# Attention and two MLPs on one core: first loads cut by columns, key parts written straight into the stacked operand, other half copied

## Chip, cores, metric

The kernel runs on one core of one Trainium2 chip. The metric is the device time of one execution in microseconds (us). The four compute engines have queues of their own that run in order: TensorE (PE), VectorE (DVE), ScalarE (ACT) and GpSimd (POOL); SyncE (SP) and ACT issue the DMAs.

## What is computed

The reference, cut to what matters (two batches, eight heads, 576 positions, head size 64):

```python
q_rot, k_rot = rotate(q), rotate(k)            # rotary position encoding, half = 32
scores = scale * q_rot @ k_rot.T               # scale = 1/8
attn = softmax(scores)                          # max subtracted first
x = (attn @ v) as [1152 tokens, 512]
h = x @ w_in;  x = (h * sigmoid(h)) @ w_out     # 2048 wide
for e in range(4):                              # 1024 wide each
    out += p[:, e] * (relu(x @ w1[e]) @ w2[e])
```

## The kernel before

All of the output has to be close to float32. A product is therefore made from two parts of each factor: a high part (the value rounded to the matmul's input type, `F32R`) and a low part (the value less its high part).

**Pairs and units.** Attention is worked in eight pairs of heads. A pair's rotated keys and queries lie as `xk` and `xq` with head 0 on partitions 0 to 63 (`TOP`) and head 1 on 64 to 127 (`LOW`). A pair has nine units (four blocks of 128 queries for each head, and one block for the rest of both). A unit is: `scores` into a PSUM tile `s` of which there are two; `rowmax` on DVE; `expo` on ACT; four to six transposes on PE (`transp`), copied out of PSUM by ACT, or by DVE for the units named in `EVD`; then `av` in two halves of a pair, and `norm`.

**The stacked operand.** `scores` uses `KK` and `QQ`, two of each, for pairs in turn. `QQ` holds a head's query high part on partitions 0 to 63 and its low part on 64 to 127; `KK[:, 0]` holds the key's high part on both halves of the partitions and `KK[:, 1]` its low part. So two accumulating matmuls over 128 partitions give all products of parts. The parts were first made in tiles of their own (`k2` by `key_high` on ACT and `key_low` on DVE, `q2` by `query_high` and `query_low` on POOL), and DMAs then spread them: four of 288 KB a pair into `KK` (`key_spread`, L275) and four of 144 KB into `QQ` (`query_spread`, L291), all from SP.

**The first units.** Before the first pair's stacked operand is there, its first `NUN` = 5 units use `first_scores` (L349): two plain float32 matmuls on the 64 partitions of one head, straight from `xq` and `xk`.

**Order.** It is written out by hand: `START` lists the steps ahead of the loop, `LATE` those put at a half step of it, and the loop has one step for each of the 72 units, in which `ORDER0` (first pair), `ORDER` and `ORDER2` (last two pairs) give the order of atoms: S scores and M rowmax of the unit two ahead, E exponential of the next, T and H transposes, L the DVE copy, B the `av` and `norm` work named in `PLAN`, W and w pieces of a weight conversion (`WIDE`). `OFF`, `OFF1` (pair 1) and `OFF2` (pair 2) give the half step at which each pair's preparation is put: `lk`, `lq`, `lv` loads; `k1` to `k3` and `q1` to `q3` the rotary; `k4`, `k5`, `q4`, `q5` the parts. `DV0` and `DV1` say which of these run on DVE and not on POOL in the first two pairs.

Ahead of everything PE runs 13 matmuls on a zero tile (L956). The MLPs follow the attention; the change leaves their code as it is.

Of the kernel before, what the change touches and what calls it, by code (L numbers as in the profile page):

```python
# [11 lines left out]
ALU = mybir.AluOpType  # L12
AX = mybir.AxisListType

PLAN = [['L0'], ['L1'], ['Ln'], [], ['P0'], [], [], ['P1', 'Pn'], []]
PLAN0 = [[], [], [], [], [], ['P0'], ['P1'], ['Pn'], []]
PLAN2 = [['L0'], [], ['L1', 'Ln'], [], ['P0'], [], [], [], ['P1', 'Pn']]
ORDER = ['vSEVTwMHXWBL', 'SBTHEwvVXWML', 'SMvXVEwTHWBL', 'vBSWTVEMHXLw', 'STVHMEwBvXWL', 'SVvEwXMWTBHL', 'ETSVwvMHXWLB', 'VTSMvWHEXLBw', 'SWTEHXvMLwBV']
ORDER0 = ['XETSHvWVMBLw', 'SVETXwMvBWHL', 'TwSvHWEXBVLM', 'SvXMWVTBHLEw', 'TVvHBXWSMwEL', 'vVEXBwSTHLWM', 'EvTHLSWwBVMX', 'VTSEvHMBLWwX', 'WwXSTBHMELvV']
ORDER2 = ['SvEMXTBHLWVw', 'vWSTMBHLEwXV', 'TvXESwWVMHLB', 'BEvSTVXMHWwL', 'TWVwSMHLEBvX', 'VELXwSBvWTMH', 'TEwBSHXvVMLW', 'TSHLEVMwWvXB', 'vBESMVWTHXwL']  # L20
WIDE = [[6, 10, 12, 14, 16, 17, 19], [18, 22, 24, 26, 28, 29, 32], [32, 35, 37, 39, 42, 44, 46], [42, 46, 48, 50, 51, 52, 55]]
# [4 lines left out]
OFF = {'k1': -28, 'k2': -27, 'k3': -25, 'k4': -19, 'k5': -16, 'q1': -20, 'q2': -26, 'q3': -19, 'q4': -18, 'q5': -14, 'lk': -42, 'lq': -35, 'lv': -5}  # L26
OFF1 = {'k1': 4, 'k2': 4, 'k3': 6, 'k4': 6, 'k5': 6, 'q1': 0, 'q2': 4, 'q3': 5, 'q4': 6, 'q5': 7, 'lv': 10}
OFF2 = {'k1': 8, 'k2': 6, 'k3': 14, 'k4': 17, 'k5': 18, 'q1': 9, 'q2': 15, 'q3': 15, 'q4': 19, 'q5': 23, 'lk': 2, 'lq': 5, 'lv': 31}
DV1 = ['k1', 'k2', 'q1', 'q2', 'q3']
DVR = []  # L30
EVD = [1, 3, 8, 4]
FIRST = [0, 2, 1, 3, 4, 5, 6, 7, 8]
NUN = 5
START = ['ka', 'kb', 'qa', 's0', 'h', 's1', 'c1', 'c2', 'm0', 'l', 'qb', 'c3', 'ch', 'x0', 's2', 'm1', 'cl']
LATE = {'d': 0, 'e': 0, 'gh': 1, 'gl': 1, 'k0': 0, 'k1': 0, 'q0': 2, 'q1': 2}
DV0 = ['c1', 'c2', 'd', 'e']
# [10 lines left out]
def fused_kernel(ctx, tc, q, k, v, w_in, w_out, dprobs, w1, w2, cst, out):  # L47
# [198 lines left out]
    def rotary(P, nm, g, rows=ALL, cols=FULL):  # L246
        x = getattr(P, "x" + nm)[rows, :, cols]

        def times(z, tab):
            if P.n == 0 and nm == "k":  # L250
# [17 lines left out]
    def key_low(P, rows=ALL, cols=FULL):  # L268
        nc.vector.scalar_tensor_tensor(P.k2[rows, 1, cols], P.xk[rows, 0, cols], 0.125 if P.n else 1.0,
                                       f32(P.k2)[rows, 0, cols], ALU.mult, ALU.subtract)  # L270

    def key_spread(P, heads=(0, 1)):
        for h in heads:
            for a in range(2):
                nc.sync.dma_start(f32(KK[P.i][64 * a:64 * a + 64, :, 576 * h:576 * h + 576]),  # L275
                                  f32(P.k2[64 * h:64 * h + 64, :, :]))
            made.add((P, "k", h))
# [9 lines left out]

    def query_spread(P, heads=(0, 1), cols=FULL):
        for h in heads:
            for z in range(2):  # L290
                nc.sync.dma_start(f32(QQ[P.i][64 * z:64 * z + 64, 640 * h + cols.start:640 * h + cols.stop]),  # L291
                                  f32(P.q2[64 * h:64 * h + 64, z, cols]))
            made.add((P, "q", h))
# [14 lines left out]
    def scores(P, un):  # L308
        hf, r, h = un
        if P.n == 0 and P.units.index(un) < NUN:  # L310
            return first_scores(P, un)
        for x in ("k", "q"):
            for h_ in (0, 1) if h == 2 else (h,):
                assert (P, x, h_) in made
# [22 lines left out]
    def first_scores(P, un, nbs=(0, 1)):  # L337
# [586 lines left out]
    def attention():  # L924
# [6 lines left out]
        QA, QB, QC, QD = slice(0, 128), slice(128, 256), slice(256, 576), slice(0, 256)  # L931
        P0.xk = yp.tile([128, 2, 576], F32, name="xk")
        P0.xq = yp.tile([128, 2, 576], F32, name="xq")
        parts(P0, "k")
        parts(P0, "q")

        def load0(e, dst, src, rows, cols=FULL):
            e.dma_start(dst[rows, :, cols], src[0, 0, rows, :, cols])

        def table0(rows, cols=FULL):  # L940
            nc.scalar.dma_start(TAB[rows, :, cols], TABS[rows, :, cols])
# [37 lines left out]
        def eng(name):  # L979
# [4 lines left out]
            "ka": all_of(rotary(P0, "k", V, TOP, CA)), "kb": all_of(rotary(P0, "k", V, TOP, CB)),  # L984
            "qa": all_of(rotary(P0, "q", V, TOP, QA)),
            "h": lambda: key_high(P0, TOP), "l": lambda: key_low(P0, TOP),
            "c1": lambda: rotary(P0, "k", eng("c1"), LOW)[0](), "c2": lambda: rotary(P0, "k", eng("c2"), LOW)[1](),
            "c3": lambda: rotary(P0, "k", eng("c3"), LOW)[2](),
            "ch": lambda: key_high(P0, LOW), "cl": lambda: key_low(P0, LOW),
            "qb": all_of(rotary(P0, "q", eng("qb"), TOP, QB)),  # L990
            "d": all_of(rotary(P0, "q", eng("d"), LOW, QD)),
            "e": all_of(rotary(P0, "q", eng("e"), ALL, QC)),
            "gh": lambda: query_high(P0, g), "gl": lambda: query_low(P0, eng("gl")),
            "k0": lambda: key_spread(P0, (0,)), "k1": lambda: key_spread(P0, (1,)),
            "q0": lambda: query_spread(P0, (0,)), "q1": lambda: query_spread(P0, (1,)),
# [8 lines left out]
        def prepare(Z):  # L1004
# [8 lines left out]
            its["k4"] = lambda: (parts(Z, "k"), key_high(Z))  # L1013
            its["k5"] = lambda: (key_low(Z), key_spread(Z))
            its["q4"] = lambda: (parts(Z, "q"), query_high(Z, g))
            its["q5"] = lambda: (query_low(Z, nc.vector if "q5" in dve else g), query_spread(Z))
            its["lv"] = lambda: load_v(Z)
            at = {1: OFF1, 2: {a: n - 36 for a, n in OFF2.items()}}.get(Z.n, OFF)
            for a in ("lk", "lq", "lv", "k1", "k2", "k3", "k4", "k5", "q1", "q2", "q3", "q4", "q5"):
# [10 lines left out]
        need = ["lk<k1", "lk<k2", "k1<k3", "k2<k3", "k3<k4", "k4<k5", "lq<q1", "lq<q2", "q1<q3", "q2<q3", "q3<q4", "q4<q5"]  # L1030
        for Z in range(1, NPAIR):
# [3 lines left out]
            for a, b in (("k5", "k4"), ("q5", "q4")):  # L1035
                assert order.get((Z - 1, a), -1) <= order[Z, b]
# [3 lines left out]
            if Z > 1:  # L1040
                for a in ("k5", "q5"):
                    assert order[Z, a] > 18 * Z - 24
# [202 lines left out]
```

## Time and profile before

| | |
|---|---|
| three runs | 755.44 us median, 754.74 to 756.63 |
| profiled execution | 755.87 us, of which the span of the trace is 754.1 us |
| PE busy | 740.4 us, 98% of the span |
| DVE, ACT, POOL busy | 472.5, 302.5, 263.4 us |
| granted TensorE clock, mean | 0.981 of 2.4 GHz |
| attention | from 0 to about 160 us |

The page lists busy time of each engine, its share in 40 equal slices of the span, the granted clock of PE in the same slices, the chain of work that ended last, and groups of instructions by source line. Line numbers are those of the kernel before. Of an engine that is busy 98% of the time, the places to read are the slices where it isn't, and those in which its clock was lower. Durations below are of one profiled execution.

### The profile page before, as it was taken

The page shows a single profiled execution, that of the slowest core. Times are in us where ns is not written, and L with a number is a line of the kernel's source. Part 1 is how long each engine was busy: PE and PEld are TensorE (multiplying, and loading weights), DVE is VectorE, ACT ScalarE, POOL GpSimd, SP SyncE. Part 2 cuts the span into 40 slices and gives each one's busy share as a digit, 9 for nine tenths or more (in the row PEclk, how much of TensorE's full clock was granted, in tenths as well). Part 3 has the DMA queues.
Part 4 walks back from the last instruction along what each step waited for, and adds up shares of the span by engine and source line. Part 5 has one row for each costly group of instructions (what it writes and reads, how often), then busy time and mean ns, then how long its engine had stood idle before and what let it go on. Part 6 is the DMA issues. An engine that isn't in the chain of part 4 may idle for free.

```text
span 754.1 us, 11327 instructions
## 1 busy us (share of the span) xinstructions
PE 740.4 (98%) x4398; PEld 667.3 (88%) x4398; DVE 472.5 (63%) x878; ACT 302.5 (40%) x679; POOL 263.4 (35%) x256
## 2 busy tenths in 40 slices
PE   6999999999999999999999999999999999999998
PEld 5667777779999999999998998989989899898996
DVE  6557878667999897984574544545445454464542
ACT  2457777664425335243242331413314133242330
POOL 2748878411003103026312614226152261522600
PEclk7789999999999999999999999999999999999999
DMA  8877686611233131330110300203012030110002
GB/s 224 215 207 195 180 244 173 165 60 31 83 112 112 57 111 57 107 118 1 56 56 1 98 16 23 91 1 108 4 34 79 1 110 3 45 68 0 2 29 99
DMA packets 26759, 63.65 MB, mean 84 GB/s; under 512 B 3536, under 2 KB 4048, under 8 KB 26704
## 3 DMA queue, kind: packets, MB, share of 16 engines
q1 hardware_dynamic: 25008, 61.91, 27.2%
q10 hardware_dynamic: 1696, 1.00, 0.7%
q8 instruction: 35, 0.57, 0.3%
q14 instruction: 20, 0.16, 0.1%
HBM read 46.39 MB, written 2.36 MB: 65 GB/s over the span
## 4 chain that ended last, share of the span: by engine, by line
PE 91%; DMA 3%; DVE 2%; POOL 2%; issue 1%; ACT 0%; POOLq 0%; DVEq 0%
PE m L766 9%; PE m L765 9%; PE m L767 9%; PE m L694 7%; PE m L693 7%; PE m L692 7%; PE m L576 5%; PE m L577 4%; PE m L578 4%; PE m L601 4%; PE m L600 4%; PE m L599 4%; PE b L440 4%; PE s L323 4%; PE b L296 4%; PE m L649 1%
## 5 line engine op out<-in xcount | busy, mean ns | idle before, releaser
L771 DVE SCALAR_TENSOR_TENSOR acc<-m,dp,acc 128x512 f32<-128x512 f32 (+1 forms) x64 | 47.5, 742 | 108.1 <-PE m L767 108.1
L766 PE MATMUL m<-wl,gh 128*128 128x512 f32 (+1 forms) x292 | 113.1, 387 | 0.0
L765 PE MATMUL m<-wh,gh 128*128 128x512 f32 (+1 forms) x292 | 113.0, 387 | 0.0
L767 PE MATMUL m<-wh,gl 128*128 128x512 f32 (+1 forms) x292 | 112.7, 386 | 0.0
L713 DVE SCALAR_TENSOR_TENSOR gl<-g,gh 128x288 fp32r<-128x288 f32 x84 | 50.7, 603 | 45.0 <-ACT gh L712 43.2
L675 POOL TENSOR_TENSOR wl<-raw,wh 128x512 fp32r<-128x512 f32 x21 | 27.2, 1298 | 141.9 <-ACT wh L672 141.9
L588 POOL TENSOR_TENSOR gl<-g,gh 128x384 fp32r<-128x384 f32 x24 | 26.8, 1120 | 142.7 <-ACT gh L587 142.6
L356 DVE TENSOR_REDUCE nm<-s 128x1 f32<-128x576 f32 x72 | 54.0, 750 | 32.8 <-PE s L323 20.9
L694 PE MATMUL m<-xh,wl 128*128 128x288 f32 x224 | 66.1, 295 | 0.0
L693 PE MATMUL m<-xl,wh 128*128 128x288 f32 x224 | 66.0, 294 | 0.0
L692 PE MATMUL m<-xh,wh 128*128 128x288 f32 x224 | 65.9, 294 | 0.0
L767 PEld LDWEIGHTS m<-wh,gl 128*128 128x128 f32 x292 | 54.8, 188 | 11.3
L366 ACT ACTIVATE p<-s,nm 128x576 f32<-128x576 f32 x72 | 53.7, 746 | 27.2 <-DVE nm L356 26.3
L765 PEld LDWEIGHTS m<-wh,gh 128*128 128x128 f32 x292 | 54.8, 188 | 10.6
L599 PE MATMUL m<-gh,wh 128*128 128x384 f32 x192 | 64.1, 334 | 0.0
L600 PE MATMUL m<-gh,wl 128*128 128x384 f32 x192 | 64.1, 334 | 0.0
L601 PE MATMUL m<-gl,wh 128*128 128x384 f32 x192 | 64.1, 334 | 0.0
L766 PEld LDWEIGHTS m<-wl,gh 128*128 128x128 f32 x292 | 54.8, 188 | 10.3
L675 POOL TENSOR_TENSOR wl<-cvt,wh 128x512 fp32r<-128x512 f32 x28 | 36.2, 1294 | 69.7 <-ACT wh L672 69.7
L672 ACT CAST wh<-cvt 128x512 fp32r<-128x512 f32 x28 | 17.4, 621 | 89.4 <-DVE cvt L671 89.4
L323 PE MATMUL s<-kk,qq 128*128 128x288 f32 x236 | 48.5, 329 | 3.5 <-DMA qq<-q 3.3
L693 PE MATMUL m<-tf,wh 128*128 128x288 f32 x168 | 49.6, 295 | 0.0
(142 smaller groups left out, 1883.1 us busy)
## 6 DMA issues: line engine op xcount, KB each, us to landing
raw<-in_moe_w_dram SPq DMA_DIRECT2D x16, 1024.0 KB, 5.1
kk<-k SPq DMA_DIRECT2D x32, 288.0 KB, 4.7
raw<-in_moe_w_out_dram SPq DMA_DIRECT2D x8, 1024.0 KB, 4.9
raw<-in_moe_w_in_dram SPq DMA_DIRECT2D x6, 1024.0 KB, 5.2
qq<-q SPq DMA_DIRECT2D x32, 144.0 KB, 4.5
xk<-in_k_dram SPq DMA_DIRECT2D x7, 576.0 KB, 5.4
xq<-in_q_dram SPq DMA_DIRECT2D x7, 576.0 KB, 6.7
xv<-in_v_dram SPq DMA_DIRECT2D x8, 320.0 KB, 5.3
```

Source lines behind the costliest of these rows:

```text
L323: nc.tensor.matmul(s[:, nb, 0:288], lq, kk[:, a, c:c + 288], start=(a == 0), stop=(a == 1))
L356: nc.vector.tensor_reduce(P.nm[:, c:c + 1], s[:, :, 0:288], AX.XY, ALU.max, negate=True)
L599: nc.tensor.matmul(o, wh[:, f, ds], gh[:, cols], start=(f == 0), stop=False)
L600: nc.tensor.matmul(o, wl[:, f, ds], gh[:, cols], start=False, stop=False)
L601: nc.tensor.matmul(o, wh[:, f, ds], gl[:, cols], start=False, stop=(f == FT - 1))
L675: nc.gpsimd.tensor_tensor(lo, src(name), f32(hi), ALU.subtract)
L692: nc.tensor.matmul(ps, wh[:, k, ms], hh[:, k, cols], start=(first and k == 0), stop=False, skip_group_check=not first)
L693: nc.tensor.matmul(ps, wh[:, k, ms], hl[:, k, cols], start=False, stop=False, skip_group_check=not first)
L694: nc.tensor.matmul(ps, wl[:, k, ms], hh[:, k, cols], start=False, stop=(k == 1), skip_group_check=not first)
L765: nc.tensor.matmul(ps, gh[:, ts], wh[:, f, ds], start=(f == 0), stop=False)
L766: nc.tensor.matmul(ps, gh[:, ts], wl[:, f, ds], start=False, stop=False)
L767: nc.tensor.matmul(ps, gl[:, ts], wh[:, f, ds], start=False, stop=(f == FT - 1))
```

## The change

Four things change.

1. **First loads.** The first pair's keys, tables and queries were loaded by heads (64 partitions, all 576 columns in one row). Now each load covers 128 partitions and a piece of the columns: 288 of `xk` and of the table, 192 of `xq`, then the rest. The rotary steps of the first pair follow these pieces for both heads at once.
2. **Key parts.** `key_high` and `key_low` write straight into `KK`, each head on the half of the partitions where its rotated keys lie, as two instructions on 64 partitions where one on 128 stood. The other half is one DMA for each head inside `KK`. `spread` issues a head's key copy and its two query copies together, so a pair has two copies of 288 KB and four of 144 KB.
3. **First units.** `NUN` is 4, so the fifth unit of the first pair uses the stacked operand; the units of the first pair run in natural order.
4. **Order.** `PLAN`, `ORDER`, `WIDE`, `OFF` and `START` have new numbers. `EVD` gets unit 7, whose transposes (and those of the fifth column block) DVE now copies instead of ACT.

```diff
-NUN = 5
+NUN = 4
-START = ['ka', 'kb', 'qa', 's0', 'h', 's1', 'c1', 'c2', 'm0', 'l', 'qb', 'c3', 'ch', 'x0', 's2', 'm1', 'cl']
-LATE = {'d': 0, 'e': 0, 'gh': 1, 'gl': 1, 'k0': 0, 'k1': 0, 'q0': 2, 'q1': 2}
+START = ['ka', 'qa', 'kb', 's0', 's1', 'm0', 'qc', 's2', 'm1', 'x0']
+LATE = {'qb': 0, 'h': 0, 'l': 0, 'gh': 0, 'gl': 0, 'sp': 2}
-EVD = [1, 3, 8, 4]
+EVD = [1, 3, 8, 4, 7]
...
-    def key_high(P, rows=ALL, cols=FULL):
-        nc.scalar.activation(P.k2[rows, 0, cols], P.xk[rows, 0, cols], AF.Copy, scale=0.125 if P.n else 1.0)
+    def key_high(P):
+        for h in range(2):
+            rows = (TOP, LOW)[h]
+            nc.scalar.activation(KK[P.i][rows, 0, 576 * h:576 * h + 576], P.xk[rows, 0, :], AF.Copy,
+                                 scale=0.125 if P.n > 1 else 1.0)
...
+    def spread(P):
+        for h in range(2):
+            k_ = f32(KK[P.i][:, :, 576 * h:576 * h + 576])
+            nc.sync.dma_start(k_[(LOW, TOP)[h]], k_[(TOP, LOW)[h]])
+            for z in range(2):
+                nc.sync.dma_start(f32(QQ[P.i][64 * z:64 * z + 64, 640 * h:640 * h + 576]),
+                                  f32(P.q2[64 * h:64 * h + 64, z, :]))
+            made.add((P, "spread", h))
...
-        load0(nc.sync, P0.xk, k, TOP)
-        table0(TOP)
-        load0(nc.sync, P0.xq, q, TOP)
-        load0(nc.scalar, P0.xk, k, LOW)
-        nc.sync.dma_start(idn, cst[:, 1152:1280])
-        table0(LOW)
-        load0(nc.sync, P0.xq, q, LOW)
+        load0(P0.xk, k, CA)
+        table0(CA)
+        load0(P0.xq, q, QA)
+        table0(CB)
+        load0(P0.xk, k, CB)
+        nc.scalar.dma_start(idn, cst[:, 1152:1280])
+        load0(P0.xq, q, QR)
```

In the rows below, a name with a number is one buffer: `kk_114`, `qq_112` are the stacked operands of even pairs, `kk_115`, `qq_113` those of odd ones, `k_...` and `q_...` tiles of parts, `b` a PSUM bank, `p` the exponentials.

**ACT, from its first instruction that isn't a DMA**, with what each waits for (`DMAHW` is the landing of a DMA, the other names are engines). Before:

```order
L266 ACT_TABLE_LOAD [waits DMAHW1_49]
L266 ACTIVATE k_120<-xk 64x576 [waits DVE_49]
L266 ACTIVATE k_120<-xk 64x576 [waits DMAHW2_49,Pool_49]
L366 ACTIVATE p,sm_110<-s,nm 128x576 [waits DVE_49] x2
L404 COPY pt<-b 128x4x128 [waits PE_49]
```

Now:

```order
L367 ACT_TABLE_LOAD [waits DVE_49]
L367 ACTIVATE p,sm_110<-s,nm 128x576 [waits Pool_49]
L269 ACTIVATE kk_114<-xk 64x576 [waits DMAHW4_49,DMAHW1_49]
L269 ACTIVATE kk_114<-xk 64x576
L367 ACTIVATE p,sm_110<-s,nm 128x576 [waits DVE_49]
L405 COPY pt<-b 128x4x128 [waits PE_49]
```

The table load stood ahead of a key part and waited for a DMA; it now stands ahead of the first exponential and waits for DVE. The key parts moved behind that exponential.

**PE, from the first scores to the first units on the stacked operand.** Before:

```order
L349 MATMUL s<-xk,xq 128x288 x4
L296 MATMUL b<-cs,p 128x128 x4
L349 MATMUL s<-xk,xq 128x288 x4
L296 MATMUL b<-cs,p 128x128 x8
L349 MATMUL s<-xk,xq 128x288 x2
L323 MATMUL s<-kk_114,qq_112 128x288 x4
L296 MATMUL b<-cs,p 128x128 x10
```

Now:

```order
L350 MATMUL s<-xk,xq 128x288 x4
L298 MATMUL b<-cs,p 128x128 x4
L350 MATMUL s<-xk,xq 128x288 x4
L298 MATMUL b<-cs,p 128x128 x8
L324 MATMUL s<-kk_114,qq_112 128x288 x8
L298 MATMUL b<-cs,p 128x128 x10
```

The fifth unit's two plain matmuls became four on the stacked operand, which then has to be there for the fifth unit and not for the sixth.

**SP, the copies of the first two pairs.** Before:

```order
L275 DMA kk_114<-k_120 64x2x576 x4
L291 DMA qq_112<-q_121 64x576 x4
L236 DMA xk<-in_k_dram 128x1152
L236 DMA xq<-in_q_dram 128x1152
L275 DMA kk_115<-k_252 64x2x576 x4
L291 DMA qq_113<-q_259 64x576 x4
```

Now:

```order
L282 DMA kk_114<-kk_114 64x2x576
L284 DMA qq_112<-q_120 64x576 x2
L282 DMA kk_114<-kk_114 64x2x576
L284 DMA qq_112<-q_120 64x576 x2
L237 DMA xk<-in_k_dram 128x1152
L237 DMA xq<-in_q_dram 128x1152
L282 DMA kk_115<-kk_115 64x2x576
L284 DMA qq_113<-q_247 64x576 x2
L282 DMA kk_115<-kk_115 64x2x576
L284 DMA qq_113<-q_247 64x576 x2
```

A pair has six copies instead of eight, and head 0's query copies now stand ahead of head 1's key copy.

## Rows read from the trace of the kernel before

**Rows 1.** Four stretches: length, busy time by engine (instructions), PEclk, DMA share, GB/s.

```profile
9.86:16.99 7.13, 5.32 (x13) 3.24 (x13) 5.73 (x10) 2.93 (x6) 1.71 (x2) 0.50 0.92 281
16.99:29.62 12.63, 12.63 (x38) 9.12 (x38) 10.18 (x18) 4.39 (x10) 5.93 (x5) 0.50 0.73 200
...
36.00:38.90 2.90, 0.00 (x0) 0.03 (x1) 0.00 (x0) 0.55 (x2) 2.82 (x3) 1.00 1.03 275
38.90:46.60 7.70, 7.48 (x34) 5.35 (x34) 4.23 (x9) 4.02 (x10) 1.31 (x3) 0.57 0.43 148
```

**Rows 2.** Longest waits of PE in the span: total us, times, longest us.

```profile
PE s L349 <- DVE xq L258: 3.4, 1, 3.4
PE s L323 <- DMA qq<-q: 3.3, 2, 3.0
```

**Rows 3.** Two more stretches, columns as in rows 1.

```profile
11.00:14.00 3.00, 3.00 (x7) 1.65 (x5) 1.99 (x3) 0.99 (x2) 1.39 (x1) 0.50 1.01 395
2.00:6.00 4.00, 4.00 (x22) 4.00 (x21) 0.00 (x0) 0.00 (x0) 0.00 (x0) 1.00 0.99 227
```

**Rows 4.** DMA issues of the first microsecond: queue, KB, us from issue to landing.

```profile
xk<-in_k_dram SPq DMA_DIRECT2D x1, 288.0 KB, 5.3
cs<-in_cst_dram ACTq DMA_DIRECT2D x1, 288.0 KB, 3.9
```

**Rows 5.** Timeline of the start: start us, duration us, engine, line, operation.

```profile
6.08 1.28 ACT L266 ACT_TABLE_LOAD   x1 [6.08 <-DMA xk<-in_k_dram]
6.12 0.82 DVE L251 SCALAR_TENSOR_TENSOR xk<-xk,cs 64x288 f32<-64x288 f32 x2 [5.08 <-DMA xk<-in_k_dram]
...
8.60 0.74 DVE L253 TENSOR_TENSOR xq<-xq,cs 64x128 f32<-64x128 f32 x2
8.67 0.68 ACT L266 ACTIVATE k<-xk 64x576 fp32r<-64x576 f32 x1 [1.31 <-DVE xk L258]
...
9.86 4.21 PE L349 MATMUL s<-xk,xq 64*128 64x288 f32 x8 [3.37 <-DVE xq L258]
...
13.69 0.74 ACT L366 ACTIVATE p<-s,nm 128x576 f32<-128x576 f32 x1
...
14.57 1.11 PE L296 MATMUL b<-cs,p 128*128 128x128 f32 x4 [0.51 <-ACT p L366]
...
18.39 1.03 POOL L283 TENSOR_SCALAR q<-xq 128x576 fp32r<-128x576 f32 x1 [5.44 <-DVE xq L258]
...
25.21 1.33 PE L323 MATMUL s<-kk,qq 128*128 128x288 f32 x4
```

**Rows 6.** Landing of copies of the first pair (3.5, 2.7) and second (6.6).

```profile
kk<-k SPq DMA_DIRECT2D x1, 288.0 KB, 3.5
...
qq<-q SPq DMA_DIRECT2D x1, 144.0 KB, 2.7
...
qq<-q SPq DMA_DIRECT2D x1, 144.0 KB, 6.6
```

**Rows 7.** Timeline at the turn from the first pair to the second.

```profile
30.64 1.44 POOL L286 TENSOR_TENSOR q<-xq,q 128x576 fp32r<-128x576 f32 x1
...
38.90 0.77 PE L323 MATMUL s<-kk,qq 128*128 128x288 f32 x4 [3.04 <-DMA qq<-q]
...
44.71 2.31 PE L440 MATMUL b<-pt,xv 128*64 128x320 f32 x8
...
47.69 1.30 PE L440 MATMUL b<-pt,xv 128*64 128x320 f32 x8
```

**Rows 8.** DVE groups from 60 to 150 us (busy, mean ns), then one pair's stretch.

```profile
L356 DVE TENSOR_REDUCE nm<-s 128x1 f32<-128x576 f32 x46 | 34.4, 749 | 13.9 <-PE s L323 8.4 <-PE s L334 5.3
L410 DVE COPY pt<-b 128x512 f32<-128x512 f32 x20 | 13.6, 682 | 3.1 <-PE b L296 3.1
L269 DVE SCALAR_TENSOR_TENSOR k<-xk,k 128x576 fp32r<-128x576 f32 x5 | 4.8, 963 | 0.0
...
L412 DVE COPY p<-b 128x256 f32<-128x256 f32 x5 | 2.1, 412 | 0.0
...
73.00:90.00 17.00, 16.82 (x124) 13.18 (x126) 14.82 (x26) 12.49 (x31) 14.01 (x14) 1.00 0.64 175
```

More of the change, by code (lines that the diff above doesn't have):

```diff
@@ L249, in times @@
         def times(z, tab):
-            if P.n == 0 and nm == "k":
+            if P.n < 2 and nm == "k":
                 nc.vector.scalar_tensor_tensor(x[:, z, :], x[:, z, :], 0.125, tab[rows, cols], ALU.mult, ALU.mult)
@@ L263, in parts, with key_low @@
         setattr(P, nm + "2", t)
-    def key_high(P, rows=ALL, cols=FULL):
-        nc.scalar.activation(P.k2[rows, 0, cols], P.xk[rows, 0, cols], AF.Copy, scale=0.125 if P.n else 1.0)
[L268 to L277, printed above, removed]
+    def key_high(P):
[3 more added lines that the diff above has]
+                                 scale=0.125 if P.n > 1 else 1.0)
+    def key_low(P):
+        for h in range(2):
+            rows = (TOP, LOW)[h]
+            hi, lo = (KK[P.i][rows, z, 576 * h:576 * h + 576] for z in range(2))
+            nc.vector.scalar_tensor_tensor(lo, P.xk[rows, 0, :], 0.125 if P.n > 1 else 1.0, f32(hi),
+                                           ALU.mult, ALU.subtract)
+    def spread(P):
+        for h in range(2):
+            k_ = f32(KK[P.i][:, :, 576 * h:576 * h + 576])
[4 more added lines that the diff above has]
+            made.add((P, "spread", h))
     def query_high(P, g, rows=ALL, cols=FULL):
@@ L286, in query_low @@
         g.tensor_tensor(P.q2[rows, 1, cols], P.xq[rows, 0, cols], f32(P.q2)[rows, 0, cols], ALU.subtract)
[L288 to L293, printed above, removed]
     def tr(o, lhsT, n=128):
@@ L309, in scores @@
         hf, r, h = un
-        if P.n == 0 and P.units.index(un) < NUN:
+        if P.n < 2 and P.units.index(un) < (NUN, NUN1)[P.n]:
             return first_scores(P, un)
-        for x in ("k", "q"):
-            for h_ in (0, 1) if h == 2 else (h,):
-                assert (P, x, h_) in made
+        for h_ in (0, 1) if h == 2 else (h,):
+            assert (P, "spread", h_) in made
         s = psS.tile([128, 2, 512], F32, name="s")
@@ L1012, in prepare @@
                     its[a] = lambda nm=nm, j=j, e=nc.vector if a in dve else g: rotary(Z, nm, e)[j]()
-            its["k4"] = lambda: (parts(Z, "k"), key_high(Z))
-            its["k5"] = lambda: (key_low(Z), key_spread(Z))
+            its["k4"] = lambda: key_high(Z)
+            its["k5"] = lambda: key_low(Z)
             its["q4"] = lambda: (parts(Z, "q"), query_high(Z, g))
-            its["q5"] = lambda: (query_low(Z, nc.vector if "q5" in dve else g), query_spread(Z))
+            its["q5"] = lambda: (query_low(Z, nc.vector if "q5" in dve else g))
+            its["sp"] = lambda: spread(Z)
             its["lv"] = lambda: load_v(Z)
             at = {1: OFF1, 2: {a: n - 36 for a, n in OFF2.items()}}.get(Z.n, OFF)
-            for a in ("lk", "lq", "lv", "k1", "k2", "k3", "k4", "k5", "q1", "q2", "q3", "q4", "q5"):
+            for a in ("lk", "lq", "lv", "k1", "k2", "k3", "k4", "k5", "q1", "q2", "q3", "q4", "q5", "sp"):
                 if a in its:
@@ L1034, in attention @@
                 assert order.get((Z, a), -1) <= order[Z, b]
-            for a, b in (("k5", "k4"), ("q5", "q4")):
-                assert order.get((Z - 1, a), -1) <= order[Z, b]
+            assert order.get((Z - 1, "sp"), -1) <= order[Z, "q4"]
             if Z > 2:
@@ L1040, in attention @@
             if Z > 1:
-                for a in ("k5", "q5"):
+                for a in ("k4", "sp"):
                     assert order[Z, a] > 18 * Z - 24
```

59 lines of the change are left out of this document (26 added, 33 removed).

## Prediction

> **What bounds the kernel now.** PE is busy 98% of the span, so I asked first where the other 2% are and where its clock is low. The list of PE's waits [rows 2] has two entries that count, 3.4 and 3.3 us, both in the first 40 us. The table of stretches [rows 1] adds the clock: from 9.86 to 29.62 PE runs at 0.50 of 2.4 GHz, that is 1.2 GHz; from 36.00 to 38.90 it does nothing; and soon after it starts again the clock is low once more (0.57 in the mean up to 46.60). The same eight matmul records of `av` take 2.31 us in that stretch and 1.30 us after it [rows 7], a factor of 1.78; four score matmuls take 1.33 and 0.77 us [rows 5, 7], a factor of 1.73. From 46.6 us on PE has work at the full clock, as the 16.82 of 17.00 us of a later pair show [rows 8]. A change ahead of that point moves the end by what it moves that point; one behind it counts only if it makes PE wait.
>
> **First loads.** Before, each load filled 64 partitions and all ran at 227 GB/s in sum (2 to 6 us); later loads on 128 partitions ran at 395 GB/s [rows 3]. Now all first loads are on 128 partitions, but in rows of 768 to 1536 bytes instead of 4608. The rate has these two rows as its ends; I take 310 GB/s, the middle, since rows a quarter as long should cost part of it. The table landed at 0.74 + 3.9 = 4.6 us and the keys 1.4 us later [rows 4]; two pieces of 295 kB at 227 GB/s are 2.6 us, so the flow began at 2.0. At 310 GB/s the same two pieces take 1.9 us: 3.9, and with the same lag of 1.4 the first rotary step starts at about 5.4 (ends: 4.4 and the old 6.1). The 192 query columns (197 kB at half the rate) follow by 6.6, the second half of the keys by 8.5, the other queries by 10.4.
>
> **First units.** A rotary triple on 288 columns takes 1.24 us (two from 6.12 to 8.60), one on 128 columns 1.26 [rows 5]; partitions don't count, so both heads cost what one did. `ka` and `qa` end at 8.0, `kb`, from 8.6, at 9.9. PE makes its first matmul at 8.1 instead of 9.86, but the other three wait for `kb`: at the low clock (4.21 us for four [rows 5]) they end at 13.1 instead of 14.07. So of 1.8 us gained only 1.0 is left here.
>
> **Table load.** Before, ACT loaded its table from 6.08 to 7.36, under the wait for data [rows 5]. Now the load waits for the first row maximum (11.8), and the exponential comes 1.28 us later; with 0.74 for it and some 0.2 for its sum the first transposes start at 14.2. They take 1.1 us, to 15.2 [rows 5]. Alongside, DVE does the second maximum (0.75 [rows 8], from 13.2) and `qb` (1.2), which ends at 15.1; so the load costs nothing beyond what `qb` costs anyway, and with that cover gone 1.28 us.
>
> The Trainium skill, page "ScalarE: Activation LUTs", section "What ACT_TABLE_LOAD costs", has the 1.28 us of the row and 1.38 us more for a drain. By the page the transposes would end 1.4 us later, and the gain below would be 4.1 us instead of 5.5.
>
> The next two units (4.21 us) end at 19.4, two groups of transposes at 21.6.
>
> **The stacked operand of the first pair.** It is wanted a unit earlier. ACT makes the high parts from 14.1 (two of 0.68, to 15.5), DVE the low ones behind `qb` (two of 0.75, to 16.6). POOL has three steps on 256 columns (2.3 us, an estimate from the 1.44 us of 576 [rows 7]), the query's high part (1.03 [rows 5]) from 15.2 and its low part (1.44) to 17.6. SP issues head 0's key copy at 16.0 and its last query copy at 17.7; with 3.5 and 2.7 us to landing [rows 6] head 0 is there at 20.4, head 1 at 22.2. PE comes to it at 21.6, and to the second unit at 23.2 behind the fourth exponential, so both are covered, by 1 us. That second unit, the sixth, ends at 24.5; before, it began at 25.21 and took 1.33 [rows 5]: 2.0 us gained, of which 0.8 come from the fifth unit (1.3 instead of 2.1).
>
> **The turn to the second pair.** Before, 12.4 us passed from there to the second pair's first scores at 38.90, of which 3.04 were the wait for a query copy [rows 7]: POOL had ended the low part at 32.08, and a copy issued then took 6.6 us to land [rows 6], behind four key copies. Now there are two key copies. `key_low` ends at 26.0 and POOL, one step earlier in everything, at 28.3; head 0's last copy is issued at 28.4. With the mean of the light and the loaded landing, (2.7 + 6.6) / 2 = 4.6 us, it lands at 33.0. PE can't use all of that: at the higher clock it outruns DVE and ACT, whose maximum and exponential are 0.75 + 0.94 us a unit, and I find it at the second pair at 35.2, which is 3.7 us ahead of before. The DMA wait is then gone; with 6.6 us to landing head 0 comes at 35.0, still just in time.
>
> **The second low stretch.** Without the 2.9 us of nothing PE has no reason that these rows show to fall back. A mean of 0.57 over 7.70 us is 6.6 us at the half clock, of which PE was busy 7.48 / 7.70 [rows 1], 6.4 us. That work now takes 6.4 / 1.73 = 3.7: 2.7 us more. Sum up to 46.6: 3.7 + 2.7 = 6.4 us.
>
> **Later pairs.** Each has one more low part on DVE (0.96 us mean [rows 8]) and the two copies of unit 7, 0.68 + 0.41, moved from ACT: 2.05 us more for DVE. ACT gets one high part (0.68) and loses copies that DVE does in about the same time, so it is no fuller. DVE stood at 14.82 of 17.00 us in its fullest pair [rows 8], so it would be at 16.87: it just fits, as long as it waits little. The high part now waits for PE's last scores out of the same `KK`; behind it on ACT stands the last unit's exponential, which is needed some 3.7 us after those scores and can be there after 0.68 * 2 + 0.94 = 2.3. The copies lose 576 KB a pair. I take 0.15 us of new waits a pair, six pairs, 0.9 us; the ends are 0 and 0.5 a pair (3 us).
>
> **Sum.** 6.4 - 0.9 = 5.5 us from the profiled 755.87 (span 754.1 and 1.8 around it) gives 750.4; the median of the runs lies 0.43 under that profiled run, so 749.9, say 750.0.
>
> **Rivals.** (a) *The loads come no sooner and the low clock returns.* With the old 227 GB/s `ka` starts at 6.1 and `kb` at 10.3, the second pair is reached at 37.2, and if its copies take the loaded 6.6 us PE waits there again and runs low for the next 6.6 us. The time from the sum is then 3 to 1 us better than before, less 0.9 for later pairs: 753 to 755, middle 754. For it: the rows are shorter. Against: 395 GB/s beside 227, and half the key copies.
>
> (b) *The clock doesn't fall at all.* PE's rest ahead of the first scores was 3.37 us [rows 5] and is 1.6 now, then 1.3. If PE is still at 2.4 GHz, the first units are no longer 1.05 us a matmul, the sixth unit ends at 22 and the second pair starts at 32.7: 2.5 us better than the forecast, 747.4. Against: it fell before, and there is only one matmul in that gap.
>
> (c) *Slower: DVE becomes the bound of the later pairs.* Maxima stand in DVE's queue behind the low parts, PE's next transposes wait for them through ACT. It decides from 6.4 / 6 = 1.1 us lost a pair. If both low parts are held up by a POOL instruction of 1.44 us, they cost 2 * 2.19 - 0.96 = 3.4 us more than the one before, and the fullest pair needs 14.82 + 3.4 + 1.1 = 19.3 us of DVE in 17.0. At 1.5 us a pair: 9.0 - 6.4 = 2.6 slower, 758.0. For it: POOL is busy 14.01 of 17.00 us there. Against: the five low parts of the steady stretch took 0.96 us in the mean, so most were not held up.
>
> The Trainium skill, page "SBUF — State Buffer", section "Who interferes with whom", gives this as a rule: a DVE instruction with two SBUF inputs and a GpSimd instruction that reads SBUF exclude each other for the whole instruction. By that rule every low part that meets POOL pays up to a whole POOL instruction, which is case (c).
>
> **How the numbers follow.** The measurement tells about 0.3% from no change, that is 753.2 and 757.7. Forecast 0.66 (747.5 to 752.5), (a) 0.13, (b) 0.15, (c) 0.06. Faster: 0.64 + 0.15 + a little of (a) = 0.81; slower 0.05, most of (c); same 0.14. The range goes from (b), 747.0, to the upper middle of (a), 754.5, and leaves out (c) and the last of both sides.
>
> **What would show it.** First DVE step at 4.4 to 6.1 us; table load behind the first maximum; sixth unit's scores done at about 24.5; no wait of PE for `qq` ahead of the second pair; no low clock behind 30 us; DVE at 15 to 16 us in a 17 us pair with PE still above 16.7. I am wrong if PE's clock is low behind 35 us, if a pair in the steady stretch takes over 17.5 us, or if the first loads land at the old times.

## The result, and the profile after

The changed kernel takes 749.50 us (median of four runs, 748.88 to 750.43), the kernel before 756.04 (754.74 to 757.52): a ratio of 0.9914, 95% interval 0.9891 to 0.9937, 6.5 us faster. The profiled run takes 748.88 us with a span of 747.1, 7.0 less than the profiled run of before. PE is busy 735.1 us (740.4 before), DVE 483.6 (472.5).

Four stretches of the changed kernel, columns as in [rows 1]:

```profile
7.14:10.00 2.86, 1.98 (x8) 0.97 (x8) 1.72 (x4) 0.00 (x0) 1.18 (x2) 1.00 1.05 415
10.00:12.58 2.58, 0.01 (x1) 0.00 (x1) 1.67 (x5) 2.17 (x4) 1.62 (x3) 0.57 0.50 206
12.58:27.20 14.62, 12.64 (x44) 9.46 (x46) 13.41 (x18) 7.68 (x16) 9.02 (x6) 0.50 0.71 189
27.20:46.60 19.40, 19.09 (x137) 14.40 (x134) 14.69 (x29) 13.34 (x30) 13.95 (x14) 0.99 0.75 199
```

The first scores now run at 2.4 GHz. The clock falls to 1.2 GHz while PE stands idle between 10.00 and 12.58 (at about 10.35, worked out from the granted clock in slices of 1 us; the expectations below say 10.65), and is back at 2.4 at about 27.4. From 27.20 to 46.60 it is 0.99 in the mean: the second low stretch of [rows 1] is gone, and so is the stretch of 2.9 us in which PE did nothing.

The longest waits of PE up to 60 us (total, times, longest), against [rows 2]:

```profile
PE b L298 <- ACT p L367: 2.8, 2, 2.6
PE s L324 <- DMA qq<-q: 1.8, 2, 1.4
...
PE s L350 <- DVE xk L259: 0.9, 1, 0.9
```

The timeline of the changed kernel, against [rows 5, 7] (start, duration, engine, line, operation; in brackets the wait ahead of it and what ended it):

```profile
4.73 0.83 DVE L252 SCALAR_TENSOR_TENSOR xk<-xk,cs 128x288 f32<-128x288 f32 x2 [3.69 <-DMA xk<-in_k_dram]
...
7.14 0.75 PE L350 MATMUL s<-xk,xq 64*128 64x288 f32 x2 [0.18 <-DVE xq L259]
8.77 1.24 PE L350 MATMUL s<-xk,xq 64*128 64x288 f32 x6 [0.88 <-DVE xk L259]
...
10.40 1.28 ACT L367 ACT_TABLE_LOAD   x1 [10.40 <-DVE nm L357]
...
11.42 0.29 DVE L259 TENSOR_TENSOR xq<-xq 128x128 f32<-128x128 f32 x1
11.70 0.74 ACT L367 ACTIVATE p<-s,nm 128x576 f32<-128x576 f32 x1
...
12.58 1.11 PE L298 MATMUL b<-cs,p 128*128 128x128 f32 x4 [2.57 <-ACT p L367]
...
13.62 3.37 PE L350 MATMUL s<-xk,xq 64*128 64x288 f32 x8
...
19.70 1.30 PE L324 MATMUL s<-kk,qq 128*128 128x288 f32 x4 [0.34 <-DMA qq<-q]
...
22.43 1.30 PE L324 MATMUL s<-kk,qq 128*128 128x288 f32 x4 [1.44 <-DMA qq<-q]
22.72 2.01 DVE L276 SCALAR_TENSOR_TENSOR kk<-xk,kk 64x576 fp32r<-64x576 f32 x2
24.00 2.00 POOL L254 TENSOR_TENSOR xk<-xk,cs 128x576 f32<-128x576 f32 x1 [0.65 <-DMA xk<-in_k_dram]
...
32.98 0.77 PE L324 MATMUL s<-kk,qq 128*128 128x288 f32 x4
```

The last row is the second pair's first scores. They wait for nothing and start 5.92 us ahead of 38.90 [rows 7].

The table follows the gain through the kernels: first scores, second pair's first scores, and the scores of the ninth unit of the second and of the last pair, each from the timeline of the profiled run. Gains are medians against the kernel before in the same set of runs.

| kernel | us (range) | gain | first | pair 2 | pair 2, ninth | last, ninth |
|---|---|---|---|---|---|---|
| before | 756.04 (754.74 to 757.52) | | 9.86 | 38.90 | 56.65 | 163.03 |
| changed | 749.50 (748.88 to 750.43) | 6.5 | 7.14 | 32.98 | 47.97 | 154.85 |
| e9_again, the same | 749.35 (748.55 to 749.89) | 6.7 | 7.73 | 34.52 | 49.52 | 156.46 |
| e1_halves | 752.34 (752.21 to 752.62) | 3.9 | 8.79 | 37.89 | 52.89 | 159.65 |
| e4_loads_alone | 756.04 (754.02 to 757.86) | 0.2 | 9.97 | 39.22 | 55.01 | 165.03 |
| e8_loads_order | 755.68 (754.57 to 756.89) | 0.3 | 7.23 | 38.32 | 54.67 | 162.69 |
| e7_copies_alone | 752.74 (750.91 to 753.01) | 3.3 | 10.33 | 38.41 | 53.16 | 159.90 |
| e12_both | 751.72 (751.60 to 752.26) | 4.4 | 7.64 | 37.07 | 51.82 | 158.83 |
| e3_copies | 752.03 (751.74 to 753.50) | 4.2 | 7.49 | 35.99 | 51.84 | 158.61 |
| e11_evd | 754.14 (752.55 to 755.40) | 2.0 | 7.81 | 33.88 | 49.19 | 159.88 |
| e2_table | 749.74 (749.61 to 750.57) | 6.5 | 8.24 | 34.55 | 49.55 | 156.48 |
| e5_fill | 749.32 (749.28 to 749.46) | 6.7 | 7.30 | 34.22 | 49.23 | 156.19 |
| e6_six | 749.75 (749.02 to 750.46) | 6.3 | 7.26 | 33.02 | 49.61 | 156.55 |
| e10_all | 746.74 (746.18 to 746.89) | 9.4 | 7.34 | 31.01 | 46.01 | 152.90 |

In the changed kernel the gain is 8.68 us at the second pair's ninth unit and 8.18 at the last pair's; the last DVE instruction starts 8.17 us earlier (750.66 and 742.49). Behind its end the span runs on for 3.0 us before and 4.1 after, 2.9 to 3.3 in all the others, so 1.2 us of this profile's gain is lost in the last output transfer of this one execution. Of the kernel before there is one profile, and its runs in all the sets span 753.66 to 758.28 us, so gains below about 1 us are not told from nothing here.

### The profile page after: what moved, and what is told of

The parts are those of the page before. It is cut to its first block, busy times and chain, and to the rows that moved or that the text cites. A ratio compares the mean times of both kernels' runs of the same rounds, so it can differ in the third digit from the quotient of the medians.

```text
span 747.1 us, 11305 instructions
## 1 busy us (share of the span) xinstructions
PE 735.1 (98%) x4398; PEld 663.9 (89%) x4398; DVE 483.6 (65%) x895; ACT 300.7 (40%) x670; POOL 266.3 (36%) x256
## 3 DMA queue, kind: packets, MB, share of 16 engines
HBM read 46.39 MB, written 2.36 MB: 65 GB/s over the span
## 4 chain that ended last, share of the span: by engine, by line
PE 93%; DVE 2%; DMA 1%; POOL 1%; ACT 1%; issue 0%; SPq 0%; ACTq 0%; DVEq 0%; POOLq 0%
PE m L767 9%; PE m L766 9%; PE m L768 9%; PE m L695 7%; PE m L694 7%; PE m L693 7%; PE b L441 5%; PE m L577 5%; PE m L578 5%; PE m L579 5%; PE m L600 4%; PE m L602 4%; PE m L601 4%; PE b L298 4%; PE s L324 4%; PE b L444 1%
## 5 line engine op out<-in xcount | busy, mean ns | idle before, releaser
L589 POOL TENSOR_TENSOR gl<-g,gh 128x384 fp32r<-128x384 f32 x24 | 26.8, 1120 | 142.7 <-ACT gh L588 142.6
L766 PEld LDWEIGHTS m<-wh,gh 128*128 128x128 f32 x292 | 54.8, 188 | 10.6
L298 PE MATMUL b<-cs,p 128*128 128x128 f32 x320 | 48.5, 285 | 2.9 <-ACT p L367 2.8
```

Of the source, the lines that this page charges most:

```text
L298: nc.tensor.matmul(o, lhsT, idn[:, 0:n], is_transpose=True, start=True, stop=True)
L766: nc.tensor.matmul(ps, gh[:, ts], wh[:, f, ds], start=(f == 0), stop=False)
```

## Experiments

### The first loads: by partition halves, alone, and with their order

e1_halves, the changed kernel with each first load cut in two:

```diff
-            nc.sync.dma_start(dst[:, :, cols], src[0, 0, :, :, cols])
+            for rows in (TOP, LOW):
+                nc.sync.dma_start(dst[rows, :, cols], src[0, 0, rows, :, cols])
```

(the table's loads likewise)

> The changed kernel, with each first load split into two transfers, one for each half of the partitions, in the same column pieces and the same order; nothing else is changed. Theory A (128 partitions in one transfer give the rate): between 2 and 6 us the rate falls from about 330 GB/s back towards the 227 GB/s of the kernel before, the first rotary step starts at 5.8 to 6.3 us instead of 4.73, the first scores start about 1.2 us later, and the whole is 1 to 1.5 us slower than the changed kernel, about 750.5. Theory B (order and size of the pieces give the early start, and the rate follows from many transfers in flight): the first rotary step still starts within 0.4 us of 4.73, and the time is within 0.5 us of the changed kernel, 749.5.

The stretch from 2 to 6 us of the changed kernel, columns as above:

```profile
2.00:6.00 4.00, 4.00 (x21) 4.00 (x20) 1.24 (x3) 0.00 (x0) 0.00 (x0) 1.00 1.01 329
```

and of e1_halves:

```profile
2.00:6.00 4.00, 3.93 (x24) 3.73 (x22) 0.00 (x0) 0.00 (x0) 0.00 (x0) 1.00 0.96 230
```

The rate falls to the 227 GB/s of before [rows 3], with the same pieces in the same order, and the DMA engines are nearly as busy (0.96 against 1.01), so it is not that the halves were issued too slowly. The first rotary step starts at 6.49, and the kernel is 2.8 us slower than the changed one, more than theory A gave: PE now rests from 5.92 to 8.79, the clock falls inside that rest (at about 8.1), and the first scores take 1.33 and 2.36 us instead of 0.75 and 1.24. So it is the 128 partitions of one transfer, not the size of the pieces. The Trainium skill gives the same advice: "DMA: Bandwidth & Descriptors", section "Rules for kernel authors", holds that two transfers to the two halves of the partitions gain nothing on each other and asks for one over all 128. The trace agrees with the advice, 230 GB/s in halves against 329.

e4_loads_alone, the kernel before with the new loads, and e8_loads_order, the same with the order of its first steps changed as well:

```diff
-START = ['ka', 'kb', 'qa', 's0',
+START = ['ka', 'qa', 'kb', 's0',
```

> The kernel before with the changed kernel's first loads alone (128 partitions, pieces of the columns); its rotary steps, key parts, copies and order are its own. Theory A (the gain of the first loads stops at the wait at the turn to the second pair, which POOL's and the copies' order sets): the first scores start 0.5 to 1.5 us earlier than 9.86, but the second pair's first scores still wait for their queries' copies and the second stretch of low clock stays; 0 to 1.5 us faster than the kernel before, 754 to 756. Theory B (the loads are what everything hangs on): the second pair starts earlier by as much as the first, and half or more of the 6.5 us is gained, below 752.8.

> The kernel before with the changed kernel's first loads and one change of its order: the first queries' rotary ahead of the second half of the keys', as in the changed kernel. Theory A (the gain of the loads ends at the turn to the second pair): the first scores start at 7.2 to 8.3 instead of 9.86, PE meets the low clock all the same, the second pair's scores start within 1 us of 38.90, and the kernel is 0 to 1.5 us faster than before, 754.5 to 756. Theory B (the start is the cause of most of the gain): the second pair's scores start 1.5 us or more earlier and 2.5 us or more are gained.

In e4 the first rotary step starts at 4.87, but `qa` still stands behind `kb` on DVE, which waits for its data, and the first scores start at 9.97, no earlier than before (theory A had them 0.5 to 1.5 us earlier): an early load is nothing without the order that uses it. In e8 they start at 7.23. Then PE waits for query copies again, at the second pair and at the third (timeline of e8_loads_order):

```profile
38.32 0.77 PE L323 MATMUL s<-kk,qq 128*128 128x288 f32 x4 [3.06 <-DMA qq<-q]
...
58.17 0.76 PE L323 MATMUL s<-kk,qq 128*128 128x288 f32 x4 [1.36 <-DMA qq<-q]
```

Of 2.63 us at the start 0.58 are left at the second pair. A shorter low stretch makes that 1.98 at its ninth unit, and the third pair's copies, 7.5 us from issue to landing, take it back. Both kernels measure the same as before (ratios 0.9997 and 0.9998; the intervals reach about 0.0015 to either side). In e8 theory A held, and there is a second wall, the third pair's copies, behind the one it named.

### The copies: alone, with the loads, and doubled again

e7_copies_alone is the kernel before with the key parts written straight into `KK` and one transfer a head; e12_both adds the edits of e8:

```diff
-            for a in range(2):
-                nc.sync.dma_start(f32(KK[P.i][64 * a:64 * a + 64, :, 576 * h:576 * h + 576]),
-                                  f32(P.k2[64 * h:64 * h + 64, :, :]))
+            k_ = f32(KK[P.i][:, :, 576 * h:576 * h + 576])
+            nc.sync.dma_start(k_[(LOW, TOP)[h]], k_[(TOP, LOW)[h]])
```

> The kernel before with the changed kernel's key parts alone: both parts written straight into the stacked operand, one transfer of 288 KB for each head to the other half of the partitions instead of two; loads, order of steps, places of the copies and number of plain units stay those of before. Theory A (the bytes of the key copies are what made the second pair's queries late): the query copies land in 3 to 4.5 us instead of 6.6, PE's wait of 3.04 us at the turn falls below 1 us, the second stretch of low clock is gone, and the kernel is 3 to 5.5 us faster than before, 750.5 to 753. Theory B (POOL's low part, which ends at 32.1, and the order on SP set it): the wait shortens by at most 1.5 us, the clock falls again behind it, and 0 to 2 us are gained, 754 to 756.

> The kernel before with both parts that were tried alone: the first loads with the first queries' rotary ahead (alone 0.3 us) and the key parts written into the stacked operand with one transfer a head (alone 3.3 us); the other steps stand in the order of before, with five plain units. Theory A (the two parts are worth more together, since an earlier start counts once the turn to the second pair doesn't wait): 5 to 6.5 us faster than before, 749.5 to 751, and the new order of steps is worth at most 1 us. Theory B (they only add up, and the new order of steps gives the rest): 3 to 4 us faster, 752 to 753.

The same place in e7_copies_alone, and the stretch behind it:

```profile
38.41 0.77 PE L330 MATMUL s<-kk,qq 128*128 128x288 f32 x4
```

```profile
34.00:47.00 13.00, 12.67 (x92) 9.67 (x91) 7.56 (x14) 10.13 (x23) 8.58 (x10) 0.99 0.68 193
```

There is no wait for copies and no second low stretch. The query copy that PE waited for at the turn, the second one of head 0, in the kernel before (issued at 33.00) and in e7_copies_alone (issued at 32.31):

```profile
qq<-q SPq DMA_DIRECT2D x1, 144.0 KB, 5.8
...
qq<-q SPq DMA_DIRECT2D x1, 144.0 KB, 3.6
```

Of the 2.9 us by which it landed earlier, 0.7 are SP's, which has two transfers less to issue ahead of it, and 2.2 are the shorter way to landing. The second pair starts only 0.5 us earlier all the same, since PE waited 0.72 us for an exponential at 28.9 and the first low stretch went on to 34. That wait is a price of the edit itself: the high part, two instructions now, holds ACT from 26.64 to 28.03 (1.39 us where one of 0.69 stood), and the exponential starts behind it at 28.06. At the second pair's ninth unit 3.49 us are gained, and 3.28 at the end, as theory A has it. In e12_both, where PE waits those 0.72 us again, the loads, worth nothing that can be told alone, add 1.1 by the medians (1.07 at the last pair's ninth unit; one of the five runs of e7 lies below all of e12's): the parts are worth more together, but 4.4 is between the two theories. So the new order of steps, with four plain units and DVE's copies of unit 7, is worth the other 2.3 us or so (4.4 to 6.7), more than theory A allowed.

e3_copies is the changed kernel with the bytes of before:

```diff
             nc.sync.dma_start(k_[(LOW, TOP)[h]], k_[(TOP, LOW)[h]])
+            nc.sync.dma_start(spare[(TOP, LOW)[h]], k_[(TOP, LOW)[h]])
```

> The changed kernel with two spare transfers of 288 KB for each pair, each a copy of a head's key parts into a tile that nothing reads, issued right behind that head's real key copy: the bytes of the copies are again those of the kernel before, and the queries' copies of that head stand behind one transfer more. Theory A (fewer bytes of copies make the operand of the second pair come in time): the second pair's first scores wait for its query copies again, start 1 to 3 us later than 32.98, and the kernel is 1.5 to 4 us slower than the changed one, 751 to 753.5; if PE is idle long enough there the granted clock falls a second time. Theory B (the earlier start and the new order of steps alone make it come in time): at the start PE waits about 0.5 to 1 us more for the first pair's operand, the second pair's scores still wait for nothing, and the time is at most 1 us over 749.5.

The longest wait of PE in e3_copies up to 60 us:

```profile
PE s L327 <- DMA qq<-q: 5.6, 3, 2.8
```

It costs 2.5 us against the changed kernel, theory A's size, but not at its place: 1.98 and 2.81 us are lost in the first pair (0.34 and 1.44 in the changed kernel), 0.80 at the second pair's second unit, and the clock does not fall again. Nor does it show bytes alone. In the first pair head 0's last query copy was issued at 17.01 instead of 16.10 and landed after 4.21 us instead of 3.46; head 1's was issued at 21.39 instead of 18.39 and landed after 3.85 in both. So most of that loss is the time that SP takes to issue, one behind another, two more transfers; at the turn, by e7, the way to landing is the larger part.

### The later pairs: unit 7's copies back on ScalarE

```diff
-EVD = [1, 3, 8, 4, 7]
+EVD = [1, 3, 8, 4]
```

> The changed kernel with unit 7's copies out of PSUM back on ScalarE (0.68 + 0.41 us a pair less on VectorE), PE's own order untouched. Theory A (VectorE's extra 2.05 us a pair are why the later pairs lose about 0.1 us each): the loss of 0.5 us between the second and the last pair goes, and the time is 0.3 to 1 us less, 748.5 to 749.2. Theory B (the new order counts on those copies on VectorE, and ScalarE's exponentials stand behind them now): PE waits for exponentials in each pair, 0.1 to 0.6 us a pair, and the time is 750 to 753.5.

From 47 to 160 us no wait of PE in the changed kernel is on the list. In e11_evd:

```profile
PE s L324 <- ACT p L367: 2.9, 5, 0.8
```

From its second pair's ninth unit to the last pair's it takes 110.69 us, the changed kernel 106.88 and before 106.38. This is theory B, and a little beyond it: 4.6 us slower than the changed kernel. With two high parts on ACT instead of one, ACT's copies of unit 7 stand ahead of exponentials that PE waits for: in one pair ACT runs the two high parts from 69.51, the two copies from 70.92 and the exponential at 71.81, and PE's scores wait 0.59 us for it, to 72.69. Those copies on DVE are a condition of the gain, not a cost beside it. (The order of the atoms is the one made for DVE's copies; one made for ACT's was not tried.)

### The first 30 us: table load, clock, plain units

e2_table puts a small exponential on ACT at the start, e5_fill seven more zero matmuls into PE's first two gaps, e6_six makes six units plain. e10_all has all three, with five zero matmuls:

```diff
+        warm = xp.tile([128, 8], F32, name="warm")
+        nc.scalar.activation(warm[:], idle[:, 0:8], AF.Exp)
...
             steps[name]()
+            for i in range({"s0": 2, "x0": 3}.get(name, 0)):
+                nc.tensor.matmul(spin, idle[:], idle[:], start=True, stop=True)
...
-NUN = 4
+NUN = 6
```

> The changed kernel, with one exponential of eight columns of a zero tile on ScalarE right behind its first DMA issues, so that the table load stands at about 1 us and not ahead of the first real exponential; its result is used by nothing. Theory A (the 1.28 us load is on the path to the first transposes, since the wait of 2.57 us of PE ends with it): the first exponential starts at about 10.4, the first transposes at about 11.3 to 11.8 instead of 12.58, and the kernel is 0.8 to 1.3 us faster than the changed one if the rest follows, about 748.4. Theory B (the prediction's: what comes next on VectorE, the second queries' rotary and the second maximum, hides it): the first transposes move but the third unit's scores do not, and the time is within 0.4 us of 749.5.

> The changed kernel with seven more matmuls of the zero tile on PE, two behind the first half of the first scores and five behind the second unit's scores, where PE waits 0.88 and 2.57 us; their result is read by nothing. Theory A (the granted clock falls at 10.65 because PE stands idle there): it stays at 2.4 GHz past 12 us, the third and fourth units' scores take about 1.7 us instead of 3.37, and since VectorE and the copies of the first pair set the pace behind them, 0.5 to 1.5 us of it reach the end: 748 to 749. Theory B (the clock falls there whatever PE does, or falls again at PE's next wait): the low stretch begins within 3 us of 10.65 all the same, and the time is 749.5 or up to 0.5 us more.

> The changed kernel with the fifth and the sixth unit of the first pair, too, as plain matmuls from the rotated keys and queries (six units so, not four), so that they don't wait for the stacked operand. Theory A (PE's waits of 0.34 and 1.44 us for the query copies are a loss at the end): at the low clock each of the two units costs about 0.4 us more than on the operand, the waits go, the ninth unit's scores start 0.7 to 1.3 us earlier than 29.50, and the kernel takes about 748.5. Theory B (VectorE, busy 6.44 of 7.00 us from 20 to 27, is what PE really follows there): the waits for the copies turn into waits for the exponentials, the ninth unit's scores start within 0.4 us of 29.50, and the time is 749.5 within 0.5 us.

> The changed kernel itself once more, for a second profile, since three kernels that differ from it only ahead of 20 us (the table load early, seven matmuls more, six plain units) came out at the same time though their scores of the second pair's ninth unit were 1.3 to 1.6 us later than in its profile. Theory A (the profile of the changed kernel was at the good end of its own spread): in this one that unit's scores start at 48.5 to 49.7 us instead of 47.97, and the end behind the last VectorE instruction takes about 3.0 us instead of 4.13. Theory B (those three edits each lost what they gained): 47.97 again within 0.3 us.

> The changed kernel with three edits together: the table load at the start, six plain units instead of four, and five more matmuls of the zero tile (two behind the first half of the first scores, three behind the second unit's). Theory A (each alone ran into the next limit, so that together they pay): the clock stays at 2.4 GHz past 15 us, the fifth and sixth units' scores don't wait, the second pair's first scores start 1 to 2 us before 32.98, and the kernel is 1 to 2 us faster than the changed one, 747.5 to 748.5. Theory B (VectorE, POOL and the second pair's copies set the pace behind 20 us whatever PE does before): PE waits at the turn to the second pair instead, and the time is 749.5 within 0.6 us.

Alone, none moves the end: 749.74, 749.32 and 749.75 beside 749.50 and 749.35.

*e2_table.* The query load landed 1.0 us later in its profiled run (5.6 us after issue, 4.6 in the changed kernel's), so the first transposes start at 12.31 instead of 12.58. The copies then hold the sixth unit (wait of 1.86 us), and the clock, back at 2.4 GHz at about 20.1, falls at about 23.5 while PE waits for ACT. The time is theory B's, within 0.4 us of 749.5, but the profile shows neither theory's way to it.

*e5_fill.* The clock stays at 2.4 GHz to about 15.1, and the third and fourth units take 1.23 and 2.01 us. So in the changed kernel it fell because PE stood idle at 8 and 10 us. But the scores on the operand start at 19.74 and 22.52, as before the edit (19.70, 22.43): the copies set that time, and the earlier units only wait longer.

*e6_six.* The two waits go, the ninth unit's scores start at 29.53 (29.50), and PE waits 1.51 us for query copies inside the second pair. The place and the time are theory B's, the mechanism is not: no wait for an exponential takes the place of the two. PE works, the two units run plain at 1.2 GHz from 19.25 to 23.0, and the clock is back at about 27.9 instead of 27.4.

*e9_again* shows how far one profile can be trusted here. DVE's two low parts of the second pair and POOL's product meet, and the order decides (timeline of e9_again; the same rows of the changed kernel stand in the timeline above, at 22.72 and 24.00):

```profile
23.11 3.20 DVE L276 SCALAR_TENSOR_TENSOR kk<-xk,kk 64x576 fp32r<-64x576 f32 x2
```

```profile
24.29 1.41 POOL L254 TENSOR_TENSOR xk<-xk,cs 128x576 f32<-128x576 f32 x1 [0.55 <-DMA xk<-in_k_dram]
```

Here POOL came first (24.29, the second low part 24.37) and the low part took 1.94 us; in the changed kernel's profile DVE came first (23.98, POOL 24.00), POOL took 2.00 instead of 1.41, and DVE was done 1.2 us sooner. That is most of the 1.55 us between 47.97 and 49.52. Theory A held: 49.52, and 3.3 us behind the last DVE instruction. The same lows took 3.11 us in e2 and 3.24 in e5, so those two lost it too, and their edits did less harm than the first profile suggests.

*e10_all* is 2.6 to 2.8 us faster than the changed kernel, and 0.9878 of before (0.9863 to 0.9894). Its stretches:

```profile
11.35:23.70 12.35, 9.33 (x46) 5.79 (x48) 11.88 (x17) 7.55 (x16) 8.97 (x6) 0.99 0.75 201
23.70:26.60 2.90, 2.90 (x10) 1.76 (x11) 1.77 (x5) 0.96 (x4) 2.90 (x3) 0.50 0.67 130
```

Each edit alone ran into the next limit: first transposes at 11.35, no wait for copies in the first two pairs, and 1.2 GHz for about 3.4 us (23.4 to 26.8) instead of 17 (10.35 to 27.4). In the first of these stretches DVE is busy 11.88 of 12.35 us: it is the fullest engine there now. Theory A held, by more than it asked. One part of it is open: the second pair's two lows took 1.89 us here (3.11 to 3.24 in e9, e2 and e5), so this profile also escaped the meeting with POOL, and no run tells how much of the 2.6 to 2.8 us that is. Against the changed kernel's first profile, which was spared by the meeting too, 1.96 us are left at the second pair's ninth unit.

## Why the prediction was right, and where it was not

The forecast was 750.0; the medians are 749.5 and 749.35. The terms, with both profiles of the changed kernel (the first, then e9_again):

**First loads.** Right within its ends: 329 GB/s (310), first rotary step 4.73 and 4.70 (5.4).

**First units.** Failed: "at the low clock ... they end at 13.1". Three matmuls took 1.24 us in the first profile and 1.60 in the second, and ended at 10.0 and 10.6. The prediction had 3.2 us, from 9.9. Two things had been left out. The clock fell in the gap behind them in the first profile (10.35), within them in the second (9.7): this is half of rival (b), the clock stayed up for the first one or two units, and no longer. And units of the two heads overlap. In the kernel before, the first two units were both head 0's; now they are of the two heads in turn, on the two halves of the partitions, and the second unit's first matmul starts at 8.78, beside the one that starts at 8.77. At the low clock the third and fourth units show it by themselves, 3.37 us against 4.21 [rows 5] and, in the kernel before:

```profile
16.99 4.17 PE L349 MATMUL s<-xk,xq 64*128 64x288 f32 x8 [1.30 <-issue]
```

The fourth unit's first matmul starts at 14.71, the third's last at 15.23. The prediction took 4.21 us for these two.

**Table load.** Failed: "the load costs nothing beyond what `qb` costs". (Its terms put the first transposes at 14.0, not at 14.2; nothing hangs on that, since `qb` had 15.1.) `qb` is done at 11.71 and the exponential starts at 11.70; the 2.57 us wait of PE ends with it, the load inside. It was hidden only in a schedule in which the scores still ran until 13.1. On the path to the first transposes it is worth its 1.28 us (11.35 in e10 against 12.58). At the end it was not worth anything by itself, since the copies came next. It starts 0.02 us behind the load. By the drain of the Trainium skill ("ScalarE: Activation LUTs", section "What ACT_TABLE_LOAD costs") it would have come 1.38 us later still; the trace does not agree.

**The stacked operand.** The times were about right, 20.4 and 22.2 for the two heads, scores at 19.70 and 22.43, in part by luck: head 0's last query copy was issued at 16.10 instead of 17.7 and took 3.46 us to land instead of 2.7. That "both are covered, by 1 us" failed: PE was early and waits 0.34 and 1.44 us. So these errors of the start, about 3 us early and 1.3 late, end at the copies, and the sixth unit's scores end at 23.73 and 24.11 against 24.5. That the sum survived them is luck: its next term was a landing, not PE's work.

**The turn.** Right in kind: no wait of PE, no second low stretch; e7 shows that the copies alone do both. Its reading of the wait mixed two copies: the 6.6 us are those of the first query copy, issued at 31.55; the one that PE waited for was issued at 33.00, not 32.08, and took 5.8. Now head 0's last copy landed at 29.88 (33.0), well ahead of PE. Short in size: 3.7 us ahead was predicted, 5.9 and 4.4 came. The step that was mis-sized is PE's way from the sixth unit to the second pair, 10.7 us in the prediction, 9.25 and 10.4 measured; the two profiles differ there by the meeting of DVE and POOL.

**The second low stretch.** 2.7 us predicted; from the second pair's first scores to its ninth unit's the gain grows by 2.76 and 2.75.

**Later pairs.** 0.9 us lost predicted, 0.50 and 0.56 measured. Of ACT "it is no fuller" was right (64.66 of the 90 us from 60 to 150, 66.93 before), but the exchange behind it is no side effect: with unit 7's copies left on ACT these pairs take 3.8 us more (e11). The sum 6.4 - 0.9 became 7.1 - 0.6 in the second profile and 8.7 - 0.5 in the first, less what the end lost.

**Rival (c).** Its mechanism is in the trace, its price is not. The first pair's two lows beside POOL took 3.41 us, more than double the 0.74 us that one takes at best. In the steady stretch each takes 0.96 us in the mean, from 0.74 to 1.28 (DVE groups from 60 to 150 us, against [rows 8]):

```profile
L411 DVE COPY pt<-b 128x512 f32<-128x512 f32 x26 | 17.7, 681 | 1.0 <-PE b L298 0.9
L276 DVE SCALAR_TENSOR_TENSOR kk<-xk,kk 64x576 fp32r<-64x576 f32 x8 | 7.7, 956 | 0.1
L413 DVE COPY p<-b 128x256 f32<-128x256 f32 x10 | 4.1, 411 | 0.0
```

DVE goes from 70.77 to 76.57 us in these 90, and PE from 89.41 to 89.69: the room was there. It was tight, as the working's 16.87 of 17 us says and its sign of 15 to 16 us does not: from 65 to 82 us DVE is busy 16.55, with PE at 16.87.

**Rival (a)** fell with the loads' rate. What stays open: why the clock stays at 1.2 GHz over stretches in which PE is nearly always busy, and how the 2.3 us of the new order split among its steps (the 0.72 us wait of e7 and e12 is one that it does away with).

## What to carry to other kernels

Follow a gain at the start to the next wall before counting it: here loads worth 2.6 us at the first matmul were worth nothing that could be told at the end until the copies behind them were halved, and three small edits worth nothing alone were worth 2.7 us together. Load over all 128 partitions, and let an engine write straight into the place from which the next engine reads, so that a copy moves only the half that has to cross. Before believing a microsecond in one profile, take a second one of the same kernel.

## What the runs showed of the hardware that was not expected

The table load took 1.28 us and the next instruction started 0.02 us behind it; ahead of it, the row maximum it waited for ended at 10.32 and it started at 10.40. The Trainium skill, "ScalarE: Activation LUTs", section "What ACT_TABLE_LOAD costs", adds a drain of 1.38 us for every switch to a different set; at this load, the first and only one of the kernel, the trace shows none on either side.

Plain scores of two heads, which lie on different halves of the partitions, ran side by side on PE: two units in 3.37 us at 1.2 GHz, 4.17 and 4.21 for two units of one head.

A DVE and a POOL instruction that touch different tiles held each other up: a low part of 64x576 took 0.74 us at best and 1.94 beside POOL, and POOL's product 1.41 or 2.00, by who started first. The Trainium skill, "SBUF — State Buffer", section "Who interferes with whom", says that the order of issue decides who waits; these rows agree, and one launch has it one way, the next the other.

PE's clock came back up in e2_table at about 20.1 us, within a gap from 19.84 to 21.70, when PE had worked without a break since 12.31, and fell again at about 23.5, within the next gap.
